# Weight conversion on two engines between the first steps, other load order, d=128 weights from the free sine column, unit 1 transformed in the head

## Chip, cores, metric

The kernel runs on one core of a Trainium2 chip. The metric is the device time of one execution in microseconds (us). "Span" is the length of the one profiled execution; it is 2 to 3 us shorter than the median of the timed runs of the same kernel.

Engine names in the profile: PE is the matrix engine (TensorE), PEld its weight loads, DVE is VectorE, ACT is ScalarE, POOL is GpSimd, SP is the engine that issues most DMAs. "ACTq" is a DMA that ACT's queue issues.

## The reference

```python
# x (8, 3008, 256) f32; w_in (256, 2048); w_out (2048, 256)   (both weights are float64 in the data)
X = np.fft.fft(np.fft.fft(x, axis=1), axis=2)
h = X.real.astype(np.float32).reshape(8 * 3008, 256) @ w_in
out = np.maximum(0.01 * h, h) @ w_out
```

The kernel folds the feature transform (axis 2, length 256) into `w_in`: a cosine part and a sine part of 128 rows each, and one row more for feature frequency d=128, whose table is +1, -1, +1, ... The sequence transform (axis 1) is done on PE with tables, in 16 "units" (8 batches, even and odd output frequencies). A step is one "up" (cos and sin products with the folded weights, then DVE, ACT and POOL) and, three steps later, one "down" (products with `w_out`; `wt` are differences of `w_out` blocks that save products).

Names in the lines below: `win` and `wo` are the converted weights, `wf` is the folded `w_in`, `wn` the d=128 row of it in column form; `nyx` and `nya` are the d=128 column of x and its sums, `nyq` its sequence transform ("Nyquist"), `nb` that row spread over the partitions; `mix` is a transformed unit, made by a "butterfly" (a sum and a difference on DVE); `g` is the hidden layer and `s` are four sums of it on POOL. "Cold" means that PE runs at half rate: four products take 2.04 us and not 1.01.

## The kernel before: the parts that matter here

The float64 weights arrive as pairs of 32-bit words. Seven DVE instructions turn 128x512 of them into float32, two of them only to clamp and shift the exponent:

```python
def to_f32(dst, raw, dtype):                      # on DVE
    ...
    v.tensor_scalar(man_i, in0=hi, scalar1=0xFFFFF, scalar2=0x100000, op0=ALU.bitwise_and, op1=ALU.bitwise_or)
    v.scalar_tensor_tensor(man, in0=lo, scalar=2.0**-32, in1=man_i, op0=ALU.mult, op1=ALU.add)
    v.tensor_scalar(power_i, in0=hi, scalar1=20, scalar2=0x7FF, op0=ALU.logical_shift_right, op1=ALU.bitwise_and)
    v.tensor_scalar(power_i, in0=power_i, scalar1=896.0, scalar2=1151.0, op0=ALU.max, op1=ALU.min)      # clamp
    v.tensor_scalar(power_i, in0=power_i, scalar1=-896.0, scalar2=2.0**23, op0=ALU.add, op1=ALU.mult)   # shift
    v.scalar_tensor_tensor(power_i, in0=hi, scalar=-(2**31), in1=power_i, op0=ALU.bitwise_and, op1=ALU.bitwise_or)
    v.scalar_tensor_tensor(dst, in0=man, scalar=2.0**-20, in1=power, op0=ALU.mult, op1=ALU.mult)
```

```python
def w_in_part(f0):                                # four times
    ...                                           # load and convert two 128x512 tiles
    for w in range(2):                            # cosine and sine rows
        ...  nc.tensor.matmul(pt, lhsT=feat_sb[:, a, w * P : (w + 1) * P], rhs=win[a], ...)
    for i in range(WN // P):                      # d=128: products with one column
        for a in range(2):
            nc.tensor.matmul(pt[:, i : i + 1], lhsT=win[a][:, i * P : (i + 1) * P],
                             rhs=feat_sb[:, a, 2 * P : 2 * P + 1], ...)
    nc.scalar.copy(wn[:, ...], pt[:, 0 : WN // P])

def up(j, f):
    ...                                           # 4 cos and 4 sin products on PE
    for h in range(2):                            # d=128 comes in here: nb (a row) times wn (a column)
        nc.vector.scalar_tensor_tensor(cos[:, hs], in0=spreads[b, c][...], scalar=wn[:, ...], in1=pt[0][:, hs], ...)
    nc.vector.tensor_tensor(g[:, 0], cos, pt[1], op=ALU.add)
    nc.vector.tensor_tensor(g[:, 1], cos, pt[1], op=ALU.subtract)
    nc.scalar.activation(g, g, ACT.Lrelu)
    ...                                           # four sums s on POOL

# the head, in order: everything before the first step
nc.sync.dma_start(feat_sb, ...); load_x(0)
fold_x(0)                                         # DVE: 7 instructions on x
for n in range(4): load_tab(nc.scalar, n, 0)
for f0 in range(0, F, WN): w_in_part(f0)
nc.sync.dma_start(nyx, x_nyq)
...                                               # three small DVE sums on nyx
nyquist(0); dft(units[0], 0); dft(units[0], 1); spread(units[0])
for n in range(4): load_tab(nc.scalar, n, 1)
for f in range(0, NH, WN // D): w_out_part(f)     # convert 8 tiles, POOL makes wt
nyquist(1)
for at in range(len(steps) + lag): ...            # steps; unit 1's transforms stand in steps 12 and 20
```

Each engine works through its own queue of instructions: in these traces an instruction that waits holds up those behind it (below, a Relu on ACT that waits 2.39 us holds up two reads). The order in which the instructions of one engine stand is fixed when the program is built; the scheduler of the build moves them within what the data allow.

## Time and profile before

| | us |
|---|---|
| median of 3 runs | 2001.89 (2000.17 to 2002.79) |
| span of the profiled run | 1999.3 |
| head, until PE has no idle moment more | 97.47 |
| dense stretch, PE 100% busy | 1896.09 |
| tail | 5.74 |
| PE busy / idle over the span | 1950.6 / 48.7 |

The prediction below shows the lines. How to read them: a row of the waits is "engine tile line <- what released it: total us, times, longest us"; a row of the timeline is "start, length, engine, line, operation, out<-in, shape, count", and in brackets the idle time just before it with its releaser. One more row is needed later, of the busy time by stretch (stretch, length, then busy us of PE, PEld, DVE, ACT, POOL, the granted clock, DMA share, GB/s), the 31 us before PE's first product in the kernel before:

```profile
0.00:31.29 31.29, 0.00 (x1) 0.01 (x1) 14.96 (x19) 1.59 (x3) 0.54 (x6) 1.00 0.78 310
```

DVE is busy for 14.96 + 61.70 = 76.66 us of the 97.47 us of head.

### The profile page before, as it was taken

Reading aid. Unit: us, or ns where it says so; the run is one execution under the profiler, and the core shown is the slowest. Engines: PE = TensorE matmul, PEld = TensorE weight load, DVE = VectorE, ACT = ScalarE, POOL = GpSimd, SP = SyncE. Lnnn points to the kernel's source line nnn. Section 1 sums busy time; section 2 is a strip of 40 time slices with the busy share of each in tenths; the row PEclk is TensorE's granted clock in tenths of the full one; section 3 lists DMA queues with packets and bytes.
Section 4 is the critical chain, followed back from the end, with each engine's and each line's share of the span. In section 5 each row is a group of like instructions: output and inputs, shape, how many; then the busy total and the mean of one; then the engine's idle time right before and its main releaser. Section 6 shows DMA issues by size and latency. Waiting matters only on the chain.

```text
span 1999.3 us, 24452 instructions
## 1 busy us (share of the span) xinstructions
PE 1950.6 (98%) x8952; PEld 1691.1 (85%) x8952; DVE 1106.4 (55%) x2111; ACT 439.1 (22%) x496; POOL 1095.0 (55%) x1572
## 2 busy tenths in 40 slices
PE   3799999999999999999999999999999999999999
PEld 1488888888888888888888888888888888888888
DVE  6945654466454744557445475545644475455444
ACT  0122222222222222222222222222222222222221
POOL 0365755566455655556555475555655566455554
PEclk9899999999999999999999999999999999999999
DMA  6301000020000200002000100002000020000000
GB/s 247 101 11 74 19 21 19 11 82 22 11 19 11 92 11 19 11 22 82 11 19 21 74 19 11 29 11 82 14 18 19 11 82 21 11 19 17 16 11 21
DMA packets 23478, 70.98 MB, mean 36 GB/s; under 512 B 2480, under 2 KB 15152, under 8 KB 21312
## 3 DMA queue, kind: packets, MB, share of 16 engines
q1 hardware_dynamic: 22208, 64.80, 8.9%
q10 hardware_dynamic: 1152, 4.63, 0.6%
q8 instruction: 71, 1.16, 0.2%
q14 instruction: 47, 0.39, 0.1%
HBM read 44.71 MB, written 24.71 MB: 35 GB/s over the span
## 4 chain that ended last, share of the span: by engine, by line
PE 96%; DVE 2%; DMA 1%; issue 0%; SPq 0%; DVEq 0%
PE sum_ps L380 57%; PE sin_ps L347 16%; PE cos_ps L347 16%; PE dft_ps L291 6%; PE up_ps L260 1%; DMA xt<-in_x_dram 1%; PE up_ps L265 0%; DVE raw L240 0%; DVE raw L241 0%; DVE raw L245 0%; DVE raw L244 0%; DVE raw L243 0%; DVE xt L189 0%; DVE win L246 0%; DVE wo L246 0%; DVE raw L242 0%
## 5 line engine op out<-in xcount | busy, mean ns | idle before, releaser
L352 DVE SCALAR_TENSOR_TENSOR cos<-nb,wn,cos_ps 128x251 f32<-128x251 f32 (+1 forms) x768 | 330.9, 472 | 731.0 <-PE cos_ps L347 731.0
L362 POOL TENSOR_TENSOR s<-g 128x251 f32<-128x251 f32 (+1 forms) x384 | 294.5, 767 | 783.7 <-ACT g L358 783.7
L358 ACT ACTIVATE g<-g 128x1004 f32<-128x1004 f32 (+1 forms) x384 | 399.1, 1039 | 1347.0 <-DVE g L357 1292.3
L380 PE MATMUL sum_ps<-s,wt 128*128 128x251 f32 (+1 forms) x2304 | 550.3, 374 | 0.0
L380 PEld LDWEIGHTS sum_ps<-s,wt 128*128 128x128 f32 x2304 | 434.2, 188 | 54.5
L347 PE MATMUL sin_ps<-mix,wf 128*128 128x251 f32 (+1 forms) x1536 | 390.6, 376 | 8.7 <-DVE nyq L300 4.8
L347 PE MATMUL cos_ps<-mix,wf 128*128 128x251 f32 (+1 forms) x1536 | 389.7, 376 | 2.0 <-DVE cos L352 2.0
L380 PE MATMUL sum_ps<-g,wo 128*128 128x251 f32 (+1 forms) x1536 | 388.6, 375 | 0.0
L347 PEld LDWEIGHTS sin_ps<-mix,wf 128*128 128x128 f32 x1536 | 291.8, 190 | 44.7 <-DVE nyq L300 5.2
L380 PEld LDWEIGHTS sum_ps<-g,wo 128*128 128x128 f32 x1536 | 291.9, 190 | 40.8
L347 PEld LDWEIGHTS cos_ps<-mix,wf 128*128 128x128 f32 x1536 | 292.3, 190 | 37.2 <-DVE cos L352 2.7
L365 POOL TENSOR_TENSOR s<-g,s 128x251 f32<-128x251 f32 (+1 forms) x384 | 275.1, 716 | 30.1
L363 POOL TENSOR_TENSOR s<-s,g 128x251 f32<-128x251 f32 (+1 forms) x384 | 291.4, 759 | 0.0
L356 DVE TENSOR_TENSOR g<-cos,sin_ps 128x502 f32<-128x502 f32 (+1 forms) x384 | 260.1, 677 | 50.5 <-DVE cos L352 10.5
L357 DVE TENSOR_TENSOR g<-cos,sin_ps 128x502 f32<-128x502 f32 (+1 forms) x384 | 257.4, 670 | 0.0
L364 POOL TENSOR_TENSOR s<-g 128x251 f32<-128x251 f32 (+1 forms) x384 | 253.0, 659 | 0.0
L380 PE MATMUL sum_ps<-s,wo 128*128 128x251 f32 (+1 forms) x768 | 225.2, 375 | 0.0
L380 PE MATMUL sum_ps<-g,wt 128*128 128x251 f32 (+1 forms) x768 | 225.2, 375 | 0.0
L380 PEld LDWEIGHTS sum_ps<-s,wo 128*128 128x128 f32 x768 | 145.6, 190 | 17.0
L380 PEld LDWEIGHTS sum_ps<-g,wt 128*128 128x128 f32 x768 | 145.9, 190 | 16.5
L291 PE MATMUL dft_ps<-tab,xt 128*128 128x377 f32 (+1 forms) x384 | 126.7, 479 | 0.0
L291 PEld LDWEIGHTS dft_ps<-tab,xt 128*128 128x128 f32 x384 | 72.6, 189 | 43.0 <-issue 0.6
(42 smaller groups left out, 434.3 us busy)
## 6 DMA issues: line engine op xcount, KB each, us to landing
xt<-in_x_dram SPq DMA_DIRECT2D x16, 1536.0 KB, 6.5
out_dram<-o SPq DMA_DIRECT2D x80, 251.0 KB, 2.3
tab<-in_seq_tab_dram ACTq DMA_DIRECT2D x8, 565.5 KB, 11.8
raw<-in_w_in_dram SPq DMA_DIRECT2D x8, 512.0 KB, 4.0
raw<-in_w_out_dram SPq DMA_DIRECT2D x8, 512.0 KB, 3.7
out_dram<-o SPq DMA_DIRECT2D x16, 250.0 KB, 2.1
nb<-nyq_dram SPq DMA_DIRECT2D x8, 376.5 KB, 3.5
nb<-nyq_dram SPq DMA_DIRECT2D x8, 376.0 KB
```

Of the source, the lines that this page charges most:

```text
L260: nc.tensor.matmul(pt, lhsT=feat_sb[:, a, w * P : (w + 1) * P], rhs=win[a], start=(a == 0), stop=(a == 1))
L291: nc.tensor.matmul(ps_t[0:m, 0 : KW[c]], lhsT=z_of(i), rhs=tabs[n, c][:, i, 0 : KW[c]], start=(i == 0), stop=(i == NI - 1))
L347: nc.tensor.matmul(pt[blk][:, h * n : (h + 1) * n], lhsT=wf[:, blk, fs], rhs=mixed[b, c][blk][:, at : at + n], start=True, stop=True)
L352: nc.vector.scalar_tensor_tensor(cos[:, hs], in0=spreads[b, c][:, at : at + n], scalar=wn[:, h * NH + f : h * NH + f + 1], in1=pt[0][:, hs ...
L356: nc.vector.tensor_tensor(g[:, 0], cos[:, 0 : 2 * n], pt[1][:, 0 : 2 * n], op=ALU.add)
L357: nc.vector.tensor_tensor(g[:, 1], cos[:, 0 : 2 * n], pt[1][:, 0 : 2 * n], op=ALU.subtract)
L358: nc.scalar.activation(g, g, ACT.Lrelu)
L362: nc.gpsimd.tensor_tensor(s1, a[1][0], a[1][1], op=ALU.add)
L363: nc.gpsimd.tensor_tensor(s2, s1, a[0][0], op=ALU.subtract)
L364: nc.gpsimd.tensor_tensor(s3, a[0][0], a[1][0], op=ALU.subtract)
L365: nc.gpsimd.tensor_tensor(s4, a[0][1], s2, op=ALU.subtract)
L380: nc.tensor.matmul(sums[j][p], lhsT=still[p], rhs=moving[p], start=(f == 0 and i % 2 == 0), stop=(f == NH - 1), skip_group_check=True)
```

## The change

Its intent: start PE earlier and keep it fed while DVE converts weights. Clamp and shift of the exponent go to ACT as two Relus; half of `w_in` and most of `w_out` is converted between the first steps; the d=128 row is put into column 0 of the sine table, which was all zero, so that it comes out of the fold and is then carried through DRAM into the column form that `up` needs; unit 1's transforms move to the head; loads are issued in another order and on other queues. With this come four buffers for the converted `w_in` tiles in place of two, and other buffers for the raw words.

```diff
 def feat_tables():
-    out[:, 2 * P :] = nyq
+    out[:, P : P + 1] = nyq
...
-        v.tensor_scalar(power_i, in0=power_i, scalar1=896.0, scalar2=1151.0, op0=ALU.max, op1=ALU.min)
-        v.tensor_scalar(power_i, in0=power_i, scalar1=-896.0, scalar2=2.0**23, op0=ALU.add, op1=ALU.mult)
+            nc.scalar.activation(power, power_i, ACT.Relu, scale=-1.0, bias=inf[:, 0:1])
+            nc.scalar.activation(power_i, power, ACT.Relu, scale=-(2.0**23), bias=inf[:, 1:2])
...
-        pt = up_ps()
-        for i in range(WN // P):
-            for a in range(2):
-                nc.tensor.matmul(pt[:, i : i + 1], ...)
-        nc.scalar.copy(wn[:, f0 // P : f0 // P + WN // P], pt[:, 0 : WN // P])
+    def spread_wn(f0):
+        row = wn_dram[:, f0 : f0 + WN]
+        nc.scalar.dma_start(row..., wf[0:1, 1]...)
+        def rest():
+            for h in range(2):
+                nc.scalar.dma_start(wn[:, h * NH + at : ...], row[h].rearrange("(q p) -> p q", p=P))
+        return rest
...
-                    dft(units[n + 1], part - 1)
+                elif n > 0:
+                    dft(units[n + 1], part - 1)()
...
+    w0 = load_w_in(0)
+    t0 = load_x(0, nc.scalar)
+    nc.scalar.dma_start(nyx, x_nyq)
+    nc.sync.dma_start(feat_sb, ...)
+    w2 = load_w_in(2 * WN)
+    for n in range(4): load_tab(nc.sync, n, 0)
+    convert(w0); fold_w_in(0, w0)
+    fold_rows(t0, 0); fold_rows(t0, 1); fold_halves(0, t0); fold_nyquist()
+    nyquist(0)(); dft(units[0], 0)(); spread(units[0]); dft(units[0], 1)()
+    convert(w2); fold_w_in(2 * WN, w2); spread_wn(0)()
+    step(0); step(1); step(2)
+    o = load_w_out(0); convert(o); combine_w_out(0)
+    w = load_w_in(WN); convert(w); fold_w_in(WN, w)
+    step(3)
+    ...                                           # last w_in part, unit 1's tables
+    spread_wn(WN)(); nyquist(1)(); spread(units[1])
+    dft(units[1], 0)(); dft(units[1], 1)()
+    for f in range(WB, NH, WB):
+        o = load_w_out(f); convert(o); combine_w_out(f)
+        step(3 + f // 2)
+    for at in range(7, len(steps) + lag): step(at)
```
(cut, and several calls drawn together on one line)

## The prediction

> **What bounds the kernel now.** I read the page first, then the busy time by stretch, the chain of waits in the head, the timeline of the first 110 us and its DMA view. The page, cut to engine shares, slices and the chain:
>
> ```profile
> PE 1950.6 (98%) x8952; PEld 1691.1 (85%) x8952; DVE 1106.4 (55%) x2111; ACT 439.1 (22%) x496; POOL 1095.0 (55%) x1572
> ...
> PE   3799999999999999999999999999999999999999
> ...
> DVE  6945654466454744557445475545644475455444
> ...
> PE 96%; DVE 2%; DMA 1%; issue 0%; SPq 0%; DVEq 0%
> ```
>
> PE is the bound at 98%, and its digits are below 9 only in the first two slices (100 us). So only the head can give time. Busy time in three stretches (columns: stretch, length, then each engine's busy us):
>
> ```profile
> 31.29:97.47 66.18, 53.28 (x177) 29.98 (x177) 61.70 (x125) 10.57 (x19) 15.27 (x19) 0.85 0.37 116
> 97.47:1993.56 1896.09, 1896.09 (x8772) 1660.38 (x8771) 1027.50 (x1963) 426.94 (x474) 1079.20 (x1548) 1.00 0.08 28
> 1993.56:1999.30 5.74, 1.25 (x6) 0.77 (x5) 2.20 (x6) 0.00 (x0) 0.00 (x0) 0.96 0.24 89
> ```
>
> The span is 97.47 of head, 1896.09 without one idle PE moment, and 5.74 of tail. In the head DVE is busy 61.70 of 66.18 us: it is the bound there. The waits of the first 100 us say for what:
>
> ```profile
> PE up_ps L260 <- DVE win L246: 33.6, 5, 31.3
> DVE xt L189 <- DMA xt<-in_x_dram: 16.3, 1, 16.3
> PE sin_ps L347 <- DVE nyq L300: 4.8, 1, 4.8
> PE sin_ps L347 <- DVE g L357: 3.9, 1, 3.9
> PE cos_ps L347 <- DVE cos L352: 2.0, 1, 2.0
> ```
>
> PE does nothing for 31.3 us (x arrives at 16.3, DVE folds it, then converts the first weights), and later waits behind DVE again: the w_out conversions stand in DVE's queue between the butterflies and the first steps. Idle PE up to 97.47 is 31.29 + 66.18 - 53.28 = 44.2 us. From the timeline, the durations I use and the cold first steps:
>
> ```profile
> 16.33 3.36 DVE L189 TENSOR_TENSOR xt<-xt 128x3072 f32<-128x3072 f32 x1 [16.33 <-DMA xt<-in_x_dram]
> 23.99 1.75 DVE L196 TENSOR_TENSOR xt<-xt 128x1536 f32<-128x1536 f32 x1
> 29.27 0.42 DVE L242 TENSOR_SCALAR raw<-raw 128x512 int32<-128x512 int32 x1
> 29.61 0.69 DVE L245 SCALAR_TENSOR_TENSOR raw<-raw 128x512 int32<-128x512 int32 x1
> 37.59 1.84 PE L265 MATMUL up_ps<-feat_sb,win 128*128 128x1 f32 x16
> 82.37 2.04 PE L347 MATMUL sin_ps<-mix,wf 128*128 128x251 f32 x4 [4.77 <-DVE nyq L300]
> ```
>
> **What the Trainium skill says.** "TensorE: Matmul & The Clock Gate", Part 1: the array runs at half rate until about 3.4 us of activity, and falls back after an idle window. The trace agrees: four passes take 2.04 us at 82.4 us, after an idle stretch, and 1.01 in the steady state. "VectorE: DVE Perf Modes", Mode 2x_2P: fp32 with one tensor source goes at twice the rate of two sources. It agrees: 0.42 against 0.69 us for 128x512. "DMA: Bandwidth & Descriptors", Queues, rings and completion order: an engine takes packets in turn from the queues that have work. It agrees: while x (SP) and tables (ACT) were both queued, the DMA records show about 25 packets of 12,288 B a microsecond from one and 22 of 4,524 B from the other. The same page, Specifications: transfers below 512 B are slow; no run so far shows 4-byte ones, which the change adds.
>
> **The change part by part.** Removed from PE: the d=128 products, 64 passes, 7.6 us of PE busy, and their PSUM bank and copies. Their weights now ride in the sine column that was always zero, so they come with the fold, but must go out to DRAM and back into 128 partitions: 2 x 512 four-byte elements for each half, ahead of the first cos. Removed from DVE: two clamping tensor_scalars per 128x512 weight tile, now two Relus on ACT (I take the 0.58 us of a 128x512 copy there); 16 tiles x 2 x 0.42 = 13.4 us less DVE. Moved: half of w_in (2 of 4 parts) and all but the first w_out conversions go behind or between the first steps; unit 1's transforms (2 x 3.8 us PE) leave steps 12 and 20 for the head. That is no gain by itself, but it is work for PE while DVE converts. The steady state has the same instructions, so its PE work stays; one step is 0.85+0.85+2.97 = 4.67 us.
>
> I now walk the new order (read from the two compiled programs) with the durations above. DVE instructions follow each other 0.08 us closer than their length: 0.34, 0.60, 0.87 (128x762 fold), 1.67.
>
> Loads: x goes first on ACT's queue, in 12,288 B packets; w_in on SP's, in 4096 B packets. Taken in turn, 8 packets per engine each, x half 0 and w0a share 2.1 MB at the measured 405 GB/s: both landed near 7.8 us; x half 1 and w0b near 13.0; then feat and nyx, w2a 15.7, w2b 17.0, four tables of 0.58 MB until 22.6.
>
> DVE: w0b's three instructions end at 14.4, fold add of half 0 at 16.1. Then stand, in this order, w2a's mask, two folds of 0.87, w2b's mask, two mantissa sums, half 1's add, and only then the last two steps of w0a and w0b: 0.34+1.74+0.34+1.20+1.67+2.40 = 7.7, so the first weights are ready at 23.8 instead of 33.1, and PE starts near 23.3 (before: 31.3). Half 1's folds, nyx and the two sums take 2x0.87+0.2+2x1.67+0.2, about 5.6: nya is there at 29.4. PE: the cold first fold took 2.08+3.99 us before, so it ends at 29.4 also; nyquist 4.1 until 33.5, two transforms of 3.9 until 41.4, the second fold 3.5 until 44.9. DVE keeps up: w2 is converted at 36.7, the second butterfly at 42.5.
>
> Then the bump: wf is copied at 45.6 on ACT, the row is written to DRAM (I take 1.7 us as for nyq_dram, 64.29 to 65.94), two ACT Relus and the DVE step they need lie between, and the two reads are issued near 50. With some 4 us for issue and landing (estimate; nb took 4.4) wn is there at 54. DVE itself reaches the first cos at 52.3, so this costs PE some 2 us; PE did steps 0 and 1 until 49.1 and idles until DVE frees a bank, near 55. DVE then needs 4 x 0.4 + 4 x 0.6 us and three conversion leftovers for two steps; PE's third step, half-rate, and fold of part 1 wait for banks until about 61.3.
>
> From there PE is fed: step 3 up 1.7 (ends 63), wait for nothing much, down 3.0, fold of part 3 3.5, nyquist 4.0, unit 1's transforms 7.6: 61.3 + 19.2 = 80.5 us. In these 19 us DVE has about 15 us of w_out conversion and butterflies, so it fits. After 80.5 the work left is the old dense stretch less one down and one unit's transforms: 1896.1 - 3.0 - 7.6 = 1885.5. Sum: 80.5 + 1885.5 + 5.7 = 1971.7 span; the median measured before is 2001.89 against 1999.3 of span, 2.6 more, so 1974.3. Check by idle: before 44.2; after 23.3 + 6 + about 3 = 32 to 33, 11 to 12 less; 7.6 less of d=128 products; some 5 less at half rate (five groups of 1.9 to 2.0 instead of 1.0 before, against two or three); rest 3 to 4 in cold folds. That sums to 27 to 28. I go to 1976, for bumps that a walk by hand overlooks.
>
> **The rivals.** First, the d=128 round trip: if 512 four-byte elements take 8 us instead of 4, or ACT stalls in issuing them, PE idles longer and all is shifted: 1980 to 1985. For it speaks that nothing else covers this time; against it that unit 0's second transform and fold lie before it. Second, DVE stays the bound through the head: POOL now combines w_out beside it, and the trace has tensor_scalars of 0.88 and 0.95 instead of 0.42 while POOL worked; the conversions of 8 w_out tiles would then push out the steps after 80 us, 5 to 8 us more. Third, loads: w0 shares the queues with x, and if it lands later than 13 us everything is shifted by as much; but DVE's order already waits for w2b at 17.0, which gives little room. Fourth, better: if wn is there at 51 and the first fold is warm, 1970.
> A gain above 2% would need 1961.9, 40 us; PE cannot start before the first weights and x (13 us) and the bump stays, so I see it as nearly excluded. Slower by 2% would need a broken steady state, for which nothing speaks.
>
> **Range and chances.** Predicted 1976 us, a gain of 26 us or 1.3%. Eight in ten: 1967 to 1986, from the first, second and fourth rival. Faster by over 2%: 0.03; within 2%: 0.96; slower by over 2%: 0.01.
>
> **What would show it.** First fold on PE at 23 to 24 us, waiting for DVE's last weight step; dense PE from about 61 us, with no idle moment to the end and a tail of 5.7; a PE gap of 5 to 6 us just before the first cos, released by DVE behind the wn DMA; two table loads on ACT, as before; PE busy about 1938 to 1945. Wrong would be: gaps between 63 and 110 us (DVE or POOL late with w_out), a first fold before 20 or after 27 us, or a changed time of the dense stretch.

## The result

| | before | after |
|---|---|---|
| median, us | 2002.34 (2000.17 to 2003.16, 4 runs) | 1979.1 (1978.76 to 1979.83, 4 runs) |
| span, us | 1999.3 | 1977.1 |
| head / dense / tail, us | 97.47 / 1896.09 / 5.74 | 87.23 / 1884.07 / 5.80 |
| PE busy / idle, us | 1950.6 / 48.7 | 1939.4 / 37.7 |

The ratio is 0.9886, with a 95% interval of 0.9869 to 0.9903. Ratios here and below are the mean time of one kernel's runs over the mean of the other's of the same rounds, so not quite the ratio of the medians.

The page after, cut in the same way but without DVE's slices:

```profile
PE 1939.4 (98%) x8888; PEld 1681.7 (85%) x8888; DVE 1103.0 (56%) x2089; ACT 460.7 (23%) x524; POOL 1092.1 (55%) x1572
...
PE   5899999999999999999999999999999999999999
...
PE 96%; DVE 3%; DMA 1%; issue 0%; ACT 0%; ACTq 0%; DVEq 0%; SPq 0%
```

The first two digits of PE went from 3 and 7 to 5 and 8: the gain lies in the first 100 us. The busy time by stretch after the change:

```profile
0.00:23.00 23.00, 0.00 (x1) 0.00 (x1) 11.62 (x20) 4.35 (x7) 0.64 (x6) 1.00 0.94 366
23.00:87.23 64.23, 53.99 (x159) 29.24 (x159) 61.37 (x102) 30.68 (x47) 25.53 (x30) 0.95 0.45 141
87.23:1971.30 1884.07, 1884.07 (x8726) 1651.59 (x8725) 1027.76 (x1964) 425.68 (x470) 1065.90 (x1537) 1.00 0.08 28
```

PE starts 8.3 us earlier, is as busy as before in the second stretch (53.99 in 64.23 us), and the dense stretch is 12 us shorter because one more "up" and "down" (4.7 us) and unit 1's transforms (7.6 us) are already done when it begins. DVE still has hardly a free moment in the second stretch (61.37 of 64.23). Over the span PE is busy for 11.2 us less (7.6 of it the 64 products for d=128, the rest products at half rate) and idle for 11.0 us less; together that is the 22.2 us.

The waits after, first 110 us, PE's rows:

```profile
PE up_ps L285 <- DVE win L262: 23.0, 1, 23.0
...
PE cos_ps L383 <- DVE cos L388: 7.7, 1, 7.7
...
PE dft_ps L318 <- DVE nyq L327: 1.7, 1, 1.7
...
PE sin_ps L383 <- DVE mix L327: 0.8, 1, 0.8
```

There are four waits, all for DVE: the first weights, then one of 7.7 us for the first cos, then two small ones. The same in the timeline of PE:

```profile
23.00 6.47 PE L285 MATMUL up_ps<-win,feat_sb 128*128 128x512 f32 x8 [23.00 <-DVE win L262]
...
44.45 1.01 PE L383 MATMUL cos_ps<-mix,wf 128*128 128x251 f32 x4
...
55.76 2.04 PE L383 MATMUL cos_ps<-mix,wf 128*128 128x251 f32 x4 [7.75 <-DVE cos L388]
...
82.43 2.17 PE L318 MATMUL dft_ps<-tab,xt 128*128 128x376 f32 x6 [1.66 <-DVE nyq L327]
...
86.28 1.11 PE L383 MATMUL sin_ps<-mix,wf 128*128 128x251 f32 x4 [0.83 <-DVE mix L327]
```

Why the first cos is late can be read from ACT, whose queue also issues the trip of the d=128 row, and from DVE. First ACT's timeline, then DVE's:

```profile
45.61 1.16 ACTq L292 DMA_DIRECT2D wn_dram<-wf  x1
...
49.93 0.72 ACT L249 ACTIVATE power<-power,inf 128x512 f32<-128x512 int32 x1 [2.39 <-DVE power L248]
50.68 0.72 ACT L250 ACTIVATE power<-power,inf 128x512 int32<-128x512 f32 x1
50.74 0.95 ACTq L297 DMA_DIRECT2D wn<-wn_dram  x2
```

```profile
48.15 0.68 DVE L260 SCALAR_TENSOR_TENSOR win<-raw,win 128x512 f32<-128x512 uint32 x1
...
54.84 1.25 DVE L388 SCALAR_TENSOR_TENSOR cos<-nb,wn,cos_ps 128x251 f32<-128x251 f32 x3 [1.02 <-issue]
```

The row is written from 45.61. The two reads stand in ACT's queue behind a Relu that waits 2.39 us for a DVE conversion, so they are issued at 50.74 and land 3.8 us later, at about 54.5. DVE idles for only 1.02 us before its first cos at 54.84: until then it converts weights of `w_in` parts and `w_out` that stand ahead of the steps in its queue.

### The profile page after: what moved, and what is told of

It is laid out like the page before. It is cut to its first block, busy times and chain, and to the rows that moved or that the text cites. A ratio compares the mean times of both kernels' runs of the same rounds, so it can differ in the third digit from the quotient of the medians.

```text
span 1977.1 us, 24341 instructions
## 1 busy us (share of the span) xinstructions
PE 1939.4 (98%) x8888; PEld 1681.7 (85%) x8888; DVE 1103.0 (56%) x2089; ACT 460.7 (23%) x524; POOL 1092.1 (55%) x1572
## 4 chain that ended last, share of the span: by engine, by line
PE 96%; DVE 3%; DMA 1%; issue 0%; ACT 0%; ACTq 0%; DVEq 0%; SPq 0%
PE sum_ps L416 57%; PE sin_ps L383 16%; PE cos_ps L383 16%; PE dft_ps L318 6%; DMA raw<-in_w_in_dram 1%; DVE power L261 0%; PE up_ps L285 0%; DVE power L248 0%; DVE wo L260 0%; DVE wo L262 0%; DVE xt L188 0%; DVE wo L247 0%; DVE cos L388 0%; DMA wn<-wn_dram 0%; DVE win L260 0%
## 5 line engine op out<-in xcount | busy, mean ns | idle before, releaser
L398 POOL TENSOR_TENSOR s<-g 128x251 f32<-128x251 f32 (+1 forms) x384 | 285.2, 743 | 797.1 <-ACT g L394 791.0
L392 DVE TENSOR_TENSOR g<-cos,sin_ps 128x502 f32<-128x502 f32 (+1 forms) x384 | 259.8, 676 | 49.6 <-DVE cos L388 11.2
L400 POOL TENSOR_TENSOR s<-g 128x251 f32<-128x251 f32 (+1 forms) x384 | 255.2, 665 | 0.0
```

Source lines behind the costliest of these rows:

```text
L392: nc.vector.tensor_tensor(g[:, 0], cos[:, 0 : 2 * n], pt[1][:, 0 : 2 * n], op=ALU.add)
L398: nc.gpsimd.tensor_tensor(s1, a[1][0], a[1][1], op=ALU.add)
L400: nc.gpsimd.tensor_tensor(s3, a[0][0], a[1][0], op=ALU.subtract)
```

## The experiments

Twelve kernels ran, on three chips: e2 to e5 on one, e1, e7 and e8 on another, the control, e9, e12, e10 and e13 on a third. The three had their own runs of the kernel before, whose medians were 2001.16, 2002.03 and 2000.95. A control, the changed kernel itself:

> The changed kernel itself again, as the control on the same chip: 1978.5 to 1980 us, first fold on TensorE at 23.0, gap of 7.7 us before the third step.

It took 1979.35 us (1978.52 to 1979.40), ratio 0.9890; its trace has the waits of 23.41, 7.72, 1.61 and 0.83 us again. Differences under about 1 us are therefore not read. The intervals of the ratios are about 3 us wide to each side, mostly by the spread of the kernel before (1999.90 to 2003.45); differences of 2 to 5 us between the kernels below are read from their own times, whose ranges are narrower, and across chips with some reserve: only the third chip had a control.

| run | edit to the changed kernel | median, us | ratio to before (95%) |
|---|---|---|---|
| e2 | clamps back on DVE | 1977.76 | 0.9886 (0.9869 to 0.9902) |
| e3 | unit 1 back in the steps | 1979.47 | 0.9891 (0.9876 to 0.9906) |
| e4 | `wn` zero, no trip (wrong result) | 1973.92 | 0.9864 (0.9850 to 0.9879) |
| e5 | no `wt` beyond the first (wrong result) | 1976.00 | 0.9875 (0.9861 to 0.9890) |
| e1 | d=128 by PE products again | 1975.06 | 0.9866 (0.9851 to 0.9881) |
| e7 | two folds of x on POOL | 1981.55 | 0.9899 (0.9882 to 0.9915) |
| e8 | old load order | 1981.71 | 0.9900 (0.9885 to 0.9914) |
| e9 | `w_in` part 2 converted after the Nyquist sums | 1979.19 | 0.9890 (0.9874 to 0.9907) |
| e12 | later conversions after the first two steps | 1977.06 | 0.9882 (0.9867 to 0.9897) |
| e10 | e1 and e9 together | 1974.28 | 0.9866 (0.9851 to 0.9880) |
| e13 | all conversions before the steps, unit 1 in the steps | 1985.90 | 0.9924 (0.9907 to 0.9940) |

### e2: is the amount of DVE work the bound?

```diff
-            nc.scalar.activation(power, power_i, ACT.Relu, scale=-1.0, bias=inf[:, 0:1])
-            nc.scalar.activation(power_i, power, ACT.Relu, scale=-(2.0**23), bias=inf[:, 1:2])
+            v.tensor_scalar(power_i, in0=power_i, scalar1=896.0, scalar2=1151.0, op0=ALU.max, op1=ALU.min)
+            v.tensor_scalar(power_i, in0=power_i, scalar1=-896.0, scalar2=2.0**23, op0=ALU.add, op1=ALU.mult)
```

> The changed kernel with the exponent clamp back on VectorE (two tensor_scalars a tile in place of two Relus on ScalarE); all else as changed. Theory D (the head is bound by VectorE's instruction time): 16 x 2 x 0.34 = 10.9 us more VectorE work, of which some 2 lie in its idle time before 12.8 us, so about 1979 + 8 = 1987 us (1984 to 1990). Rival P (the head is bound by loads and by the wn round trip, VectorE only looks busy): within 2 us of 1979.

DVE has 32 instructions more and is busy for 9.0 us more over the span (1112.0 against 1103.0), and the kernel took 1977.76 us (1977.64 to 1979.32): not slower. PE's timeline of this run:

```profile
15.70 6.00 PE L285 MATMUL up_ps<-win,feat_sb 128*128 128x512 f32 x8 [15.70 <-DVE win L262]
24.92 3.97 PE L318 MATMUL dft_ps<-tab,nyx 128*8 128x377 f32 x12 [3.21 <-DVE nyx L350]
...
49.15 2.04 PE L383 MATMUL cos_ps<-mix,wf 128*128 128x251 f32 x4 [5.62 <-DVE cos L388]
```

The build put DVE's queue in another order: without the two crossings to ACT the first weights are finished at once, so PE starts at 15.70 instead of 23.00, DVE's first cos comes at 46.83 instead of 54.84, and PE's third step 6.6 us earlier, behind a shorter gap. Later gaps of 1.26, 1.88, 0.40, 1.81 and 0.54 us take most of that back. Two things follow. Within this interleaved head, the move of the clamps to ACT brings nothing. And 7.3 us of earlier start come with less than 2 us in the end, so the start alone does not set the end. It does not show what the extra work costs at a fixed order, since the order moved with it.

### e3: the place of unit 1's transforms

```diff
-                if part == 0 and n > 0:
+                if part == 0:
...
-                elif n > 0:
+                else:
...
-    spread(units[1])
-    for blk in range(2):
-        dft(units[1], blk)()
```

> The changed kernel with unit 1's two transforms back between the steps of unit 0, as before the change. Theory F (they are TensorE work that covers VectorE's w_out conversions): TensorE idles about 4 to 5 us between 74 and 95 us instead of 2.5, so 1981 to 1983 us. Rival N (moved work, neutral): within 1 us of 1979.

1979.47 us (1978.65 to 1979.62), with gaps of 7.81, 1.69 and 0.64 us where the changed kernel has 7.75, 1.66 and 0.83. The place of unit 1's transforms is neutral as long as steps stand between the conversions: PE then does steps in that time instead.

### e4: the trip of the d=128 row taken away

Wrong: `wn` is set to zero at the start (relative error of the output 0.059).

```diff
+    nc.gpsimd.memset(wn[:, :], 0.0)
...
-    spread_wn(0)()
...
-    spread_wn(WN)()
```

> The changed kernel without the trip of the d=128 weights through DRAM: wn is set to zero, so the result is wrong on purpose. Theory T (the 7.75 us TensorE gap before the third step is the price of the trip): the gap goes, about 1979 - 7 = 1972 us. Theory D (VectorE is busy 18.8 of 20 us there, only 1.0 us of it idle, so the conversions only change places with the steps): the gap moves to a later fold or step, 1979 - 1 to - 3, so 1976 to 1978 us.

1973.92 us (1973.84 to 1974.07). The 7.75 us gap shrank to 0.44 us at 48.56, followed by 0.75, 0.94, 1.05, 0.96, 0.41 and 0.44. The trip costs 5 us, more than the low expectation of 1 to 3 and less than the high one of 7.

### e1: the trip replaced by the old products

```diff
+        pt = up_ps()
+        for i in range(WN // P):
+            for a in range(2):
+                nc.tensor.matmul(pt[:, i : i + 1], lhsT=made[a].dst[:, i * P : (i + 1) * P], rhs=feat_sb[:, a, 2 * P : 2 * P + 1], ...)
+        nc.scalar.copy(wn[:, f0 // P : f0 // P + WN // P], pt[:, 0 : WN // P])
...
-    spread_wn(0)()
...
-    spread_wn(WN)()
```
(and the feature table with its old column)

> The changed kernel with the d=128 weights made by 32 products of one column again (as before the change), no trip through DRAM. Theory D (VectorE bounds the head): their 6 to 7.6 us of TensorE time fall mostly into its idle time, and the wait for the trip goes, so within 2 us of 1979 (1977 to 1981). Rival P (TensorE time in the head counts in full): 1979 + 6 = 1985 us; rival T (the trip costs 7 us): 1979 - 7 + 6 = 1978, told from D by the wn-zero run.

1975.06 us (1974.49 to 1975.36), a correct result and 4 us faster than the change as it stands. PE is busy for 1944.5 us, 5.1 more than in the changed kernel, but the span is 1973.3: idle time fell from 37.7 to 28.8 us. The 64 products took 7.6 us before; that only 5.1 are added has to do with the rate: e1 has no cold products after its start, the changed kernel has some after the 7.75 us gap (2.04 us for four at 55.76). After the start only two PE gaps are left, 0.94 us (below) and 0.44 us at 115.92, and DVE's first cos comes at 48.82 instead of 54.84:

```profile
54.63 1.54 PE L422 MATMUL sum_ps<-s,wt 128*128 128x251 f32 x6 [0.94 <-POOL s L405]
```

```profile
48.22 0.67 DVE L260 SCALAR_TENSOR_TENSOR win<-raw,win 128x512 f32<-128x512 uint32 x1
48.82 0.84 DVE L394 SCALAR_TENSOR_TENSOR cos<-nb,wn,cos_ps 128x251 f32<-128x251 f32 x2
```

Up to that mantissa sum (L260, at 48.15 and 48.22 us) DVE runs nearly alike in both. Then the kernel with products goes to the first cos, and the changed kernel first does 9 more conversion instructions. So in this interleaved order the removed 7.6 us of products are not a gain: PE did not lack time there.

### e12 and e9: only the order of DVE's queue

Both keep every instruction and add one edge for the scheduler: "issue these after that instruction". e12 puts the conversions of the last `w_in` part and of all `w_out` tiles but the first two after the sums of step 1; e9 puts the conversion of the second `w_in` part after the first Nyquist sum.

```diff
# e12
-    convert(w)
+    with tc.issue_after(marks[0, 1].ins):        # the last DVE instruction of step 1
+        convert(w)
...
-        convert(o)
+        with tc.issue_after(marks[0, 1].ins):
+            convert(o)
# e9
-    convert(w2)
+    with tc.issue_after(first.ins):              # the first sum of nya
+        convert(w2)
```

> The changed kernel, same instructions and the same trip of the d=128 weights through DRAM; only an order edge: the conversions of the last w_in part and of the later w_out come after the first two steps in VectorE's queue. Theory O: the first cos comes near 51.5 instead of 54.8 (the reads of wn no longer stand behind Relus on ScalarE that wait for VectorE), the 7.7 us gap falls to 4 to 5, so 1976 to 1977 us. Theory T (the trip itself is the price): cos at 54.8 or within 1 us of it, gap as before, 1979.

1977.06 us (1976.88 to 1979.50): 2.3 us better by median, with one run of four at the control's level. The mechanism is plain in ACT's, DVE's and PE's timelines:

```profile
46.89 0.95 ACTq L297 DMA_DIRECT2D wn<-wn_dram  x2
```

```profile
50.70 1.63 DVE L388 SCALAR_TENSOR_TENSOR cos<-nb,wn,cos_ps 128x251 f32<-128x251 f32 x4 [2.26 <-DMA wn<-wn_dram]
```

```profile
52.01 2.04 PE L383 MATMUL cos_ps<-mix,wf 128*128 128x251 f32 x4 [4.53 <-DVE cos L388]
...
66.60 5.37 PE L285 MATMUL up_ps<-win,feat_sb 128*128 128x512 f32 x8 [2.33 <-DVE win L262]
```

No Relu of a later tile stands ahead of the reads on ACT any more, so they are issued 3.85 us earlier; now DVE truly waits for the DMA, 2.26 us, and PE's gap is 4.53 instead of 7.75 us. The conversions pushed back open a gap of 2.33 us later. So DVE waits some 2 us for the trip's own length; e12 is still 3.1 us above e4, and the rest of the 5 us lies in the order that the build chose around the trip. That order holds the first cos in DVE's queue too: in e8 below the reads went out at 48.15 us, and DVE, without waiting for them, still came to its first cos only at 54.03.

> The changed kernel, same instructions; only an order edge: VectorE takes the second weight pair (w2) after the first Nyquist sum, not ahead of the end of the first pair. Theory O (the order of VectorE's queue decides, not its amount of work): first fold near 19 instead of 23.0, Nyquist near 27.3 instead of 29.4, so about 2 us less, 1977 us. Rival W (the amount of VectorE work bounds the head): the same work, so within 0.6 of the control.

A miss: 1979.19 us (1978.48 to 1979.39). The first fold came at 22.50 us and not at 19: the build filled the place of the second pair with folds of x, which again stand ahead of the end of the first weights. And the reads of the row were issued at 50.39, as late as in the changed kernel, and the gap before the first cos grew to 8.52 us, so the little that was won at the start ran into the same wait. What an earlier end of the first weights is worth at a fixed order was not tested.

### e5: does POOL slow DVE?

Wrong (relative error 0.953): POOL makes `wt` only for the first pair of tiles, the rest is zero.

```diff
+    nc.gpsimd.memset(wt[:, :, WB:], 0.0)
...
-        combine_w_out(f)
         step(3 + f // 2)
```

> The changed kernel in which GpSimd combines w_out only for the first pair of blocks; the other combined weights are zeroed at the start, so the result is wrong on purpose. Theory C (VectorE is slowed by GpSimd working beside it, 0.95 for 0.42 and 1.2 for 0.68 us): between 72 and 88 us VectorE is back at 0.42 and 0.68, the two TensorE gaps at 80.8 and 85.4 us (1.66 and 0.83) go, 1976.5 us. Rival O (they come from the order of VectorE's queue and the waits on ScalarE): gaps stay, within 0.7 us of 1979.

1976.00 us (1975.88 to 1976.77), 3.1 us less, and the gaps at 80.8 and 85.4 us are gone. DVE's timeline, the same instructions in the changed kernel and then without POOL's subtractions:

```profile
73.04 1.23 DVE L260 SCALAR_TENSOR_TENSOR wo<-raw,wo 128x512 f32<-128x512 uint32 x1
74.19 0.95 DVE L247 TENSOR_SCALAR wo<-raw 128x512 int32<-128x512 int32 x1
```

```profile
72.98 0.68 DVE L260 SCALAR_TENSOR_TENSOR wo<-raw,wo 128x512 f32<-128x512 uint32 x1
73.58 0.41 DVE L247 TENSOR_SCALAR wo<-raw 128x512 int32<-128x512 int32 x1
```

The Trainium skill, "SBUF — State Buffer", section "Who interferes with whom", says that DVE and GpSimd share one pair of ports as an exclusive lock, that a DVE instruction with two SBUF inputs contends with a GpSimd instruction that reads SBUF, and that one in a two-port mode contends with GpSimd. This trace agrees: 1.23 against 0.68 and 0.95 against 0.41 us. Only the subtractions went: while POOL makes the sums `s`, from 62 to 72 us, DVE is as slow in e5 as in the change (0.95 and 1.22 us at 63.11 and 63.97).

### e7: folds of x moved from DVE to POOL

```diff
-    fold_rows(t0, 1)
-    fold_halves(0, t0)
+    fold_rows(t0, 1, nc.gpsimd)
+    fold_halves(0, t0, nc.gpsimd)
```
(two of the 128x1536 sums go to POOL)

> The changed kernel with two of image 0's folds (first add of its second half, the difference of the halves; 1.67 us each on VectorE) on GpSimd, which idles until 41 us. Theory D: VectorE reaches the first weights 1.7 us sooner and the Nyquist rows 3.3 us sooner, TensorE starts near 21.3, 1976 us (1975 to 1977). Rival C (GpSimd and VectorE slow each other, which gives it back): 1978.5 to 1981.

1981.55 us (1981.49 to 1981.74), 2.4 us worse. Such a sum takes 3.42 us on POOL against 1.75 on DVE, the first fold moved back to 25.21 us, and PE ran more at half rate (mean granted clock 0.66 between 45 and 65 us, against 0.83 in the change; PE busy 1942.2 against 1939.4 us).

### e8: the old load order

```diff
-    w0 = load_w_in(0)
-    t0 = load_x(0, nc.scalar)
-    nc.scalar.dma_start(nyx, x_nyq)
     nc.sync.dma_start(feat_sb, feat_tab.rearrange("(a p) n -> p a n", p=P))
+    t0 = load_x(0)
+    for n in range(4):
+        load_tab(nc.scalar, n, 0)
+    w0 = load_w_in(0)
+    nc.sync.dma_start(nyx, x_nyq)
     w2 = load_w_in(2 * WN)
-    for n in range(4):
-        load_tab(nc.sync, n, 0)
```

> The changed kernel with the loads in the order of before (feature table and x first on SP, tables on ScalarE's queue, then the weights). Theory D: VectorE starts dense work near 16.3 instead of 12.8 us, but w2's four instructions (1.9 us) then stand later, first fold near 26, 1979 + 2 = 1981 us (1980 to 1983). Rival L (the earlier first weights are the gain): TensorE starts 8 us later as before, 1987 us.

1981.71 us (1980.84 to 1982.68), 2.4 us worse than the control; the first fold still came at 23.39 us, although the first weight tile was there only at 18.63 us (7.85 in the change). The load order is a small part of the gain.

### e10: a version that beats both

e1 with the edge of e9.

> Candidate: the d=128 weights by products again (no trip) and w2 ordered after the first Nyquist sum. If the two gains add: 1975.1 - 2 = 1973 us (1972.3 to 1974.3), faster than both kernels. If VectorE's amount of work binds once the gaps are gone, 1975.

1974.28 us (1973.74 to 1974.98), correct: 4.8 us faster than the change. It has two PE gaps after the start, 0.94 and 0.44 us. Its ratio to before is the same 0.9866 as that of e1, so no gain of the edge over e1 is shown.

### e13: nothing between the conversions

No undoing of a single part had lost more than 2.6 us of the 22, so the last run put the order back as a whole: all of `w_in` and `w_out` before the first step and unit 1 in the steps, with the new conversion, the new loads and the trip kept. It differs from e3 by the interleaving alone.

```diff
     spread_wn(0)()
-    step(0)
-    step(1)
-    step(2)
-    ...                                          # steps between conversions, as in the change
+    w = load_w_in(WN); convert(w); fold_w_in(WN, w)
+    w = load_w_in(3 * WN)
+    for n in range(4): load_tab(nc.sync, n, 1)
+    convert(w); fold_w_in(3 * WN, w)
+    spread_wn(WN)()
+    for f in range(0, NH, WB):
+        o = load_w_out(f); convert(o); combine_w_out(f)
+    nyquist(1)()
+    for at in range(len(steps) + lag):
+        step(at)
```

> The changed kernel with its parts in the old arrangement: all four parts of w_in and all w_out conversions are written before the first step, and unit 1's transforms stand in the steps again (that alone was neutral: 1979.5). Conversion by DVE and ScalarE, load order and the d=128 weights from the sine place stay. It differs from the run with unit 1 in the steps by the interleaving alone. Theory I (putting steps between the conversions is what brings the bulk of the gain): the built order has some 60 conversion instructions of about 0.5 us between the second butterfly (43 us) and the end of the first cos, so DVE comes to the first steps at 73 to 77 us instead of 54; PE has the other folds, Nyquist and two half-rate steps until about 59 us, then idles 14 to 18 us where the run with unit 1 in the steps idles 10; with a cold restart 1986 to 1992. Rival (DVE's total of conversions sets when PE becomes dense, whatever stands between them): within 3 of 1979.5. First fold at 23 us in both.

1985.90 us (1985.17 to 1986.47), 6.4 us above e3. The 1986 that the theory put at the low end of its range is what came; the rival's 1982.5 is excluded. PE's timeline and the busy time up to the dense stretch:

```profile
65.62 2.04 PE L383 MATMUL sin_ps<-mix,wf 128*128 128x251 f32 x4 [6.38 <-DVE nyq L327]
73.29 2.04 PE L383 MATMUL cos_ps<-mix,wf 128*128 128x251 f32 x4 [5.62 <-DVE cos L388]
77.35 2.01 PE L383 MATMUL sin_ps<-mix,wf 128*128 128x251 f32 x4 [2.02 <-DVE g L393]
```

```profile
0.00:23.16 23.16, 0.00 (x0) 0.00 (x1) 11.61 (x20) 4.36 (x7) 0.64 (x6) 1.00 0.93 365
23.16:80.61 57.45, 43.20 (x108) 20.54 (x109) 51.30 (x92) 28.11 (x43) 17.45 (x19) 0.85 0.50 156
```

These are the three gaps of the kernel before (4.77, 1.96 and 3.91 us, on the same kinds of instruction) in about the same place in the work: PE runs out of work while DVE converts `w_out`. With the steps between the conversions, e3 has 7.81, 1.69 and 0.64 us in their place, 4 us less idle (PE is idle for 41.8 us of e13's span and 37.8 of e3's) and 1.9 us less at half rate; in the medians the interleaving is worth 6.4 us.

The other 15 us are still there in e13. Of the 15.8 us between the two profiled spans, 8.9 are PE busy time (7.6 of it the removed products) and 6.9 PE idle time. DVE's numbers say where they may lie. Until PE is dense, with the fourth "up" begun in both kernels, DVE is busy for 11.61 + 51.30 = 62.91 us in 112 instructions here, against 76.66 us in 144 in the kernel before, and the head is 97.47 - 80.61 = 16.9 us shorter. The 32 clamp instructions, at the 0.34 us in which they follow each other, are 10.9 of the 13.75 us between them; the rest is in part step work, of which the kernel before has done more at that point. And in the kernel before DVE waits 1.44, 0.78 and 0.54 us for d=128 products that still read the two buffers of `win`. So without interleaving the amount of DVE work may count after all, where e2 found no cost with interleaving. This is argued from busy times, not shown: runs of e13 with the clamps back on DVE, and with the d=128 products and two buffers back, would decide it, and were not made.

## Why the prediction was right

It said 1976 us, 1967 to 1986, and within 2%; measured were 1979.1. Its walk through the head gave the mechanism nearly throughout:

| step of the prediction | predicted | measured |
|---|---|---|
| PE starts, waiting for DVE's last weight step | 23.3 | 23.00 |
| first fold ends, Nyquist starts | 29.4 | 29.40 |
| second fold ends | 44.9 | 44.45 |
| reads of the d=128 row issued | near 50 | 50.74 |
| landing of those reads | some 4 us | 3.8 us |
| row is there for the first cos | 54 | 54.5 (cos starts at 54.84) |
| PE gap before the first cos | 5 to 6 | 7.75 |
| step 3 on PE | 61.3 | 62.74 |
| unit 1's transforms end | 80.5 | 84.44 |
| PE dense, no idle moment more | 61 | 87.23 |
| tail | 5.7 | 5.80 |
| PE busy | 1938 to 1945 | 1939.4 |
| span | 1971.7 | 1977.1 |

- **The first start** was read right from the built order: DVE finishes the first weights only behind folds and masks of other tiles, so the time at which they arrive (7.85 us for the first tile) hardly matters. e8 shows it: there the first tile is taken up at 18.63, and PE starts at 23.39.
- **"In these 19 us DVE has about 15 us of w_out conversion and butterflies, so it fits"** is the step that failed. DVE was busy without a pause from 61.5 us to the end of the Nyquist butterfly at 82.4, nearly 21 us. The same instructions at their undisturbed spacing add up to about 14 us (an estimate from 0.34 and 0.60 us and the like), so the amount was right and POOL's work beside it made it longer: without POOL's subtractions (e5) the butterfly ends at 79.8, and what is left of the slowing goes with the sums `s`. PE waited 1.66 and 0.83 us, and e5 is 3.1 us faster. These are the "gaps between 63 and 110 us" that the prediction had named as a sign of being wrong. The prediction had named this as its second rival, with the right durations (0.88 and 0.95 for 0.42), at 5 to 8 us, and then did not put any of it into the sum. The part that e5 takes away is 3.
- **"This costs PE some 2 us"**, on the trip of the row, was mis-sized: e4 and e1 show 5 and 4. The trip's own length is about the 2 us that were meant: in e12, where nothing else stands ahead, DVE waits 2.26 us for it. The rest is that the build, which seems to take the row to be late, puts 9 conversions ahead of the first cos, and that the two reads stand behind Relus in ACT's queue.
- **"16 tiles x 2 x 0.42 = 13.4 us less DVE"** counts the instructions at full length; at the prediction's own spacing of 0.34 us they are 10.9, DVE's busy time over the span fell by 3.4 us (1106.4 to 1103.0), and e2 has 9.0 more than the change. The clamps on ACT buy nothing in this order (e2). The Relu also took 0.72 us and not the 0.58 assumed. The Trainium skill, "ScalarE: Activation LUTs", section "What ACT_TABLE_LOAD costs", gives 280 ns and 0.833 ns for each element for an activation with a 128x1 bias operand, so by estimate 0.71 us for 512: the trace agrees with it, and the prediction should have taken it from there. The two table loads that the prediction expected came, 1.28 us each, as that page says.
- **"64 passes, 7.6 us of PE busy"** removed was right as busy time and no gain in this order: adding them back instead of the trip is 4 us faster (e1).
- **Unit 1's move** "is no gain by itself": right (e3, 0.1 us).
- **The sums**: "61.3 + 19.2" should read 19.8 by its own terms (1.7 + 3.0 + 3.5 + 4.0 + 7.6), 0.6 us that the reserve hid. The check by idle time came to 27 to 28 us where 22.2 were measured: its idle part was right (11 to 12; measured 11.0), its half-rate and cold part, 8 to 9 us, measured 3.6.
- **The reserve**: the walk summed to 1974.3, and 1.7 us were added for "bumps that a walk by hand overlooks". Bumps of 3 us by POOL and 2 us at the first cos came; the 2.0 us between median and span of the changed kernel were allowed for as 2.6. That the total came within 3 us is in part luck, since these errors are of either sign.

What stays open: how the 15 us that e13 keeps divide between the clamps on ACT, the removed products with the buffers of `win`, and the new order of the first loads and folds. Taken back alone in the interleaved order, the clamps, the products and the load order lose at most 2.6 us; the order of the folds was not tested alone.

## What to carry to other kernels

In this head, bound by waits, the order of VectorE's queue mattered at least as much as its amount of work once steps stood between the conversions: compare the built order of two versions engine by engine, since a build can put other work ahead of everything that needs one late operand (9 conversions here). Before work is taken off an engine, ask whether that engine lacks time there: here 7.6 us of matrix products in a stretch where PE waits were cheaper than the trip through DRAM that replaced them. And when work is put on GpSimd beside VectorE, cost the VectorE instructions beside it at their slowed length.

## What the Trainium skill lacked or had wrong

- "TensorE: Matmul & The Clock Gate", Part 1, puts the change to full rate at about 4 us into sustained activity, give or take 0.5 us. Here it varied more: it came 5.6 us after PE's first product in the change (23.00 to 28.61 us) and 2.9 us after it in e10 (22.39 to 25.31), by the clock records of the traces. "Seeing it yourself" there warns that such records can be unreliable; these two fit the weight loads, which still took 0.34 us at 28.28 in the change and 0.19 at 25.64 in e10. But the first record comes only with that change, and the profile counts the time before it as full clock: it reads 1.00 from 23.00 to 29.40 us, although the first fold took 6.47 us there and the same eight products took 3.60 us at 41.02. So take the rate at a start from the products' own lengths.
- "DMA: Bandwidth & Descriptors" says that a non-contiguous last dimension becomes one descriptor for each element, but gives no time for a transfer of that kind. Here two reads of 512 four-byte elements each landed 3.8 us after they were issued, about as long as a 512 KB load of `w_out` (3.9 us).
- "SBUF — State Buffer" has the lock between VectorE and GpSimd, but no sizes for this pair of instructions: 0.41 to 0.95 us and 0.68 to 1.23 us at 128x512.
- No page has the point that mattered most: the order of an engine's queue is fixed by the build, it seems from assumed times, so taking away a late operand moves instructions that have nothing to do with it (first cos 54.84 us in the change, 48.82 us in e1; first fold 23.00 and 15.70 us in e2).
